# Half of a first MoE product by one level of Strassen, in batches 2 to 5 of an attention + MoE kernel

## The chip, the cores and the metric

The kernel runs on one core of a Trainium2 chip. The metric is device time in microseconds (us). A core has five engines with an instruction stream each: TensorE (matmuls; the profile calls it PE, and its weight loads PEld), VectorE (DVE), ScalarE (ACT), GpSimd (POOL) and SyncE (SP, which here only issues DMAs). TensorE writes into PSUM[...]; VectorE and ScalarE read it from there.

## The reference

```python
# q, k, v: (8, 12, 448, 64);  w_in: (768, 2048);  w_out: (2048, 768)
q_n, k_n = rmsnorm(q, g_q), rmsnorm(k, g_k)
scores = q_n @ k_n.T / sqrt(64)
attn = exp(scores - max); attn = attn / (sum(attn) + 1e-9)
x = (attn @ v), laid out as (8 * 448, 768)
h = x @ w_in
g = maximum(0.01 * h, h)
return g @ w_out                      # (3584, 768) float32
```

There are eight batches of 448 tokens. The change concerns `x @ w_in`, the first product.

## The kernel before

The attention of a batch is done in three units of four heads, 24 units in all (u = 0 to 23). A unit has four steps (d = 0 to 3): in step 0 the scores of one key tile, in steps 1 to 3 of two each. Step 0 also holds the `attn @ v` product of the unit before (`pv`), its row sums (`zc`) and the shift of the exponentials (a maximum on VectorE, a matmul, a small maximum on VectorE). Between the scores, TensorE is given items of the MoE products of an earlier batch from a queue, in proportion to their estimated cost; jobs for the other engines are handed out one after each item:

```python
def fill(u, d, jobs):
    ...                       # left: the steps until this batch's queue has to be empty
    debt[0] += total * WD[d] / left
    while queue and debt[0] >= queue[0][0] * 0.5:
        c, fn = queue.pop(0)
        fn()                          # one item: TensorE's matmuls
        debt[0] -= c
        if jobs:
            jobs.pop(0)()             # one job of another engine
    flush()                           # what items left to be emitted later
    for job in jobs:
        job()
```

A batch's items enter the queue in step 3 of units 6, 9, 12, and so on: those of batch b in unit 3b + 3. The jobs that matter here:

```python
if d == 0 and narrow(u - 1): job(zcol_inv, u - 1)          # ScalarE, then DMAs
if u + 4 < NU:               job(load, u + 4)              # q and k of a later unit (step 0)
if d == 1: job(prep_g, u + 1); job(prep_ssq, u + 2, ...) x2   # VectorE
if d == 2: job(prep_rinv, u + 2)                           # ScalarE
           job(prep_norm, u + 2, ...) x2                   # VectorE, waits for rinv
           job(prep_trd, u + 2)                            # DMA transpose
if d == 3: job(prep_sq, u + 3, ...) x2                     # ScalarE
```

(This list is shortened: the conditions on u are cut.)

A block of the first product is 128 of the 2048 features: six matmuls of 448 columns into one PSUM bank, then one activation on ScalarE. Four banks are passed around. The list `held` gives the first one free, and the semaphores see to it that its last reader is done:

```python
def aux(shape, dtype, name):
    if held:
        return held[0].pop(0)
    return psum.tile(shape, dtype, tag="aux", bufs=4, name=name)

def drop(bank):
    if held:
        held[0].append(bank)

def moe1(b, ft):                                   # an item "M", cost 1.13
    xt = xts[b]
    hps = aux([P, 512], FP32, "hps")
    for kt in range(KT):                           # KT = 6
        nc.tensor.matmul(hps[:, 0:S], win16[:, kt // 2, kt % 2, ts(ft, P)], xt[:, kt // 2, kt % 2],
                         start=(kt == 0), stop=(kt == KT - 1))
    prelu(b, gt[:, ft, ...], hps[:, 0:S])          # ScalarE
    drop(hps)
```

The second product (`g @ w_out`) already uses one level of Strassen (the functions `s1` to `s4` and `seven`). For the first product only the last two batches do: batch 6 for half of its blocks, batch 7 for all. There the seven products are numbered 1 to 7, and each is done for pairs s of output blocks, as six matmuls of 224 columns (half of the tokens). What a product leaves for the other engines is put off with `later` and emitted by `flush` at the start of the next item:

```python
def item(n, s):                                    # cost 0.575
    flush()
    ...
    if n == 1:
        mm(get(1, s), 1, s, x_b(b, 0, 0), True)
        later(lambda: copy(tmp["u"][:, s % 2], g[1, s][:, 0:S]))     # a copy to SBUF
    elif n == 2:
        mm(get(2, s), 2, s, x_b(b, 1, 0), True)                      # a bank of its own
        ...
    elif n == 4:
        mm(g[7, s], 4, s, xs[4], False)            # accumulates onto what VectorE left there
        later(lambda: out_(s, 1, 0, g[7, s][:, 0:S]))                # ScalarE
        later(lambda: drop(g[7, s]))
```

## Time and profile before

| | |
|---|---|
| time, median of 3 | 421.34 us (421.13 to 421.40) |
| span of the profiled execution | 420.3 us, 9568 instructions |
| granted TensorE clock, mean | 0.992 |
| first product, 448 columns, blocks outside the very first two (L362) | 612 matmuls |
| first product by Strassen, 224 columns (L564) | 252 matmuls |
| exponentials (L214) | 166, mean 1010 ns |
| activation of a block (L356) | 556 ns |

The profile's page gives busy time by engine and the chain that ended last; the trace behind it can be asked for busy time by stretch, for the waits, and for the instructions in order of time. In a line of the timeline the first number is the start in us from the beginning of the span, the second the length, then come engine, line of the kernel, operation, and output <- inputs with their shapes; "x6" means that six instructions are merged, and a bracket at the end tells how long the engine sat idle before it and what ended that. A line such as "DVE n L167 <- ACT rinv L161: 44.2, 15, 6.6" in the list of waits says that VectorE waited for ScalarE 44.2 us in total, 15 times, 6.6 us at the longest. The end of a matmul is modelled, so that consecutive matmuls overlap in the records: the distance from one start to the next is what one costs.

### The profile page before, as it was taken

What the parts mean: (1) busy time and instruction counts of PE and PEld (TensorE: products, weight loads), DVE (VectorE), ACT (ScalarE), POOL (GpSimd) and SP (SyncE); (2) the same over time, 40 slices, a digit from 0 to 9 for tenths busy, and PEclk for the clock granted to TensorE, in tenths of its full rate; (3) what the DMA queues carried; (4) which work ended last, traced back from release to release, by engine and by line L of the source; (5) the groups of instructions that cost most, each with busy time, mean ns of one, the idle gap of its engine ahead of it and who ended that gap; (6) DMA issues with size and microseconds to landing.
All of it is one profiled execution on the core that took longest, in us unless ns stands there. A gap on an engine that the chain in (4) does not pass through costs nothing.

```text
span 420.3 us, 9568 instructions
## 1 busy us (share of the span) xinstructions
PE 404.4 (96%) x3959; PEld 222.9 (53%) x3959; DVE 269.2 (64%) x440; ACT 303.6 (72%) x474; POOL 83.0 (20%) x75
## 2 busy tenths in 40 slices
PE   7977999999999999999999999999999999999995
PEld 6544444555445544555445544455445557558853
DVE  5788665787658736466448745467338787527762
ACT  5999878868987689867986779967986657653600
POOL 1958422300020111210121111120101101010000
PEclk9699999999999999999999999999999999999999
DMA  8999999889664795678565796578562460032023
GB/s 257 218 239 237 235 250 147 200 156 215 169 153 68 224 212 120 168 163 180 152 130 107 194 203 150 151 141 170 180 111 44 121 155 11 7 78 75 2 53 100
DMA packets 71951, 62.42 MB, mean 149 GB/s; under 512 B 36324, under 2 KB 67044, under 8 KB 71908
## 3 DMA queue, kind: packets, MB, share of 16 engines
q1 hardware_dynamic: 61312, 49.62, 47.2%
q0 software_dynamic: 10272, 11.80, 18.1%
q8 instruction: 31, 0.51, 0.5%
q10 hardware_dynamic: 324, 0.39, 0.3%
q14 instruction: 12, 0.10, 0.1%
HBM read 45.61 MB, written 11.01 MB: 135 GB/s over the span
## 4 chain that ended last, share of the span: by engine, by line
PE 83%; ACT 8%; DVE 6%; issue 1%; DMA 1%; SPq 0%; DVEq 0%; ACTq 0%
PE hps L362 27%; PE sT L195 8%; PE sT L340 6%; PE ma L444 5%; PE md L444 5%; PE mc L444 5%; ACT et L214 5%; PE bank L444 5%; PE bank L564 4%; PE op L403 3%; PE zc L283 3%; PE mb L444 3%; DVE n L167 2%; PE sT L444 2%; PE bank L403 1%
## 5 line engine op out<-in xcount | busy, mean ns | idle before, releaser
L214 ACT ACTIVATE et<-sT,eb 128x896 f16<-128x896 f32 x166 | 159.4, 1010 | 18.6 <-PE sT L195 16.9
L362 PE MATMUL hps<-xt,win 128*128 128x448 f16 x600 | 120.8, 353 | 0.2 <-DVE xt L349 0.2
L362 PEld LDWEIGHTS <-win 128*128 128x128 f16 x612 | 56.8, 98 | 58.2 <-issue 9.6
L320 POOL TENSOR_TENSOR xt<-x,rz 128x896 f16<-128x896 f32 x16 | 33.4, 2085 | 148.0 <-DMA rz<-zs 139.5
L356 ACT ACTIVATE gt<-hps 128x448 f16<-128x448 f32 x100 | 54.0, 556 | 6.1 <-PE hps L362 5.4
L167 DVE TENSOR_TENSOR n<-rq,rinv 128x896 f16<-128x896 f32 (+2 forms) x25 | 27.2, 1090 | 47.0 <-ACT rinv L161 44.2
L195 PE MATMUL sT<-qkT 64*64 64x448 f16 x664 | 53.2, 369 | 3.0 <-ACT et L214 1.9
L155 DVE TENSOR_REDUCE ssq<-sq 128x14 f32<-128x896 f32 (+2 forms) x49 | 50.3, 1058 | 1.6 <-ACT sq L144 1.6
L444 PEld LDWEIGHTS <-sa 128*128 128x128 f16 x352 | 32.8, 98 | 26.3 <-issue 6.1
L295 ACT COPY x<-sT 128x896 f32<-128x896 f32 x19 | 17.2, 906 | 36.4 <-DVE sT L245 36.4
L124 POOL DMA_DIRECT2D vt<-in_v_dram x24 | 18.2, 757 | 114.9 <-PE sT L340 107.4
L444 PEld LDWEIGHTS <-gt 128*128 128x128 f16 x264 | 25.2, 98 | 18.7 <-issue 2.1
L195 PEld LDWEIGHTS <-qkT 64*64 64x64 f16 x672 | 15.2, 105 | 36.8 <-issue 33.5
L340 PE MATMUL sT<-et,vt 64*64 64x448 f16 x532 | 28.5, 350 | 0.3
L403 PE MATMUL op<-wout,gt 128*128 128x384 f16 x160 | 28.4, 327 | 0.0
L232 DVE TENSOR_REDUCE sT<-sT 128x1 f32<-128x896 f32 x22 | 24.1, 1093 | 4.3 <-PE sT L195 4.3
L340 PEld LDWEIGHTS <-vt 64*64 64x64 f16 x672 | 20.7, 107 | 11.3 <-issue 1.7
L167 DVE TENSOR_TENSOR n<-rk,rinv 128x896 f16<-128x896 f32 (+2 forms) x26 | 26.1, 1009 | 0.0
L403 PEld LDWEIGHTS <-gt 128*128 128x128 f16 x192 | 17.6, 98 | 14.3 <-issue 3.0
L444 PE MATMUL ma<-wout,gt 128*128 128x384 f16 x128 | 23.5, 326 | 0.0
L425 DVE TENSOR_TENSOR sa<-gt 128x512 f16<-128x512 f16 (+1 forms) x15 | 8.2, 544 | 18.5 <-ACT gt L356 13.9
L144 ACT ACTIVATE sq<-rq 128x896 f32<-128x896 f32 (+2 forms) x18 | 16.3, 913 | 1.3 <-DMA rq<-in_q_dram 1.3
(135 smaller groups left out, 516.6 us busy)
## 6 DMA issues: line engine op xcount, KB each, us to landing
rq<-in_q_dram SPq DMA_DIRECT2D x24, 448.0 KB, 3.9
rk<-in_k_dram SPq DMA_DIRECT2D x24, 448.0 KB, 5.6
out_dram<-ost SPq DMA_DIRECT2D x52, 192.0 KB, 3.3
rz<-zs SPq DMA_DIRECT2D x76, 112.0 KB, 2.3
vt<-in_v_dram POOLq DMA_DIRECT2D x24, 224.0 KB, 5.1
win<-in_moe_w_in_dram POOLq DMA_DIRECT2D x8, 384.0 KB, 16.8
wout<-in_moe_w_out_dram POOLq DMA_DIRECT2D x2, 1536.0 KB, 29.7
out_dram<-ost SPq DMA_DIRECT2D x4, 96.0 KB, 2.1
```

Source lines behind the costliest of these rows:

```text
L124: nc.gpsimd.dma_start(vts[u % NV].rearrange("p a t d -> p a (t d)"), rows(v, u))
L155: nc.vector.tensor_reduce(buf(u, "ssq")[:, ti, :, c[0]:c[1]], buf(u, f"sq{ti}")[:, :, c[0]:c[1]], axis=AXL.X, op=ALU.add)
L167: nc.vector.tensor_tensor(buf(u, "n16")[:, ti, c[0]:c[1]].rearrange("p s a d -> p a s d"), src[:, :, c[0]:c[1]], buf(u, "rinv")[:, ti, :, ...
L195: nc.tensor.matmul(banks[a][64 * r:64 * r + 64, 0:S].rearrange("p (t x) -> p t x", t=NS), kT(u, r, a, t), qT(u, r, a), start=True, stop=True)
L214: nc.scalar.activation(s["et"][:, t], sT[:, :, 0:S], AF.Exp, bias=s["eb"], scale=1.0)
L232: nc.vector.tensor_reduce(s["spare"][:, 511:512], sT[:, :, 0:S], axis=AXL.XY, op=ALU.max)
L320: eng.tensor_tensor(xts[b][:, g], s["x32"], s["rz"], op=ALU.mult)
L340: nc.tensor.matmul(s["pv"][r][64 * a:64 * a + 64, 0:S], vts[u % NV][64 * r:64 * r + 64, a, t], s["et"][64 * r:64 * r + 64, t, a], start=(t ...
L356: nc.scalar.activation(dst, src, AF.Prelu, bias=0.0, scale=1.0, alpha=0.01)
L362: nc.tensor.matmul(hps[:, 0:S], win16[:, kt // 2, kt % 2, ts(ft, P)], xt[:, kt // 2, kt % 2], start=(kt == 0), stop=(kt == KT - 1))
L403: nc.tensor.matmul(op2[:, 0:HC], gt[:, ft, ds(col(t), P)], wout16[:, ft, ds(HC * half, HC)], start=(ft == 0), stop=(ft == FT - 1))
L444: nc.tensor.matmul(bank[:, 0:HC], a[:, f], b[:, f], start=(first and f == 0), stop=(f == HF - 1), skip_group_check=not first)
```

## The change

In batches 2 to 5 the first product of eight of the sixteen blocks (pairs 2 and 3, in both halves of the features) is done as seven products instead of eight. The aim is to take matmul work off TensorE. The four sums of weight blocks that this needs are made once, in unit 9, and used to the end; one of them overwrites a block of the weights in place, and the other three stand in the third buffers of q, k and their squares, so that from then on those have two buffers and the loads of q and k are issued in step 2 instead of step 0. In step 3 of units 9, 12, 15 and 18 VectorE makes four sums of x, for batches 2, 3, 4 and 5.

So as not to need SBUF buffers and more than four banks, a product's values are combined in PSUM: product 1 is copied by VectorE into a bank `g[6, s]`, onto which TensorE then accumulates products 6, 5 and 3, while product 2 is accumulated onto product 1's own bank; product 7's bank takes a sum from VectorE and then product 4. [...]

```diff
+    def written():
+        for i, x in enumerate(held[0]):
+            if any(x is y for y in full):
+                return held[0].pop(i)
...
     def load(u, engines=None):
-        raw[u] = [raws.tile([P, 2, NS, D], FP32, tag=name, name=name) for name in ("rq", "rk")]
+        raw[u] = [ring(raws, name, u in (2, 5, 8), [P, 2, NS, D], FP32, name) for name in ("rq", "rk")]
...
+        def mid(n, s):
+            flush()
+            hold()
+            if n == 1:
+                mm(get(1, s), 1, s, x_b(b, 0, 0), True)
+                later(lambda: g.__setitem__((6, s), written()))
+                later(lambda: nc.vector.tensor_copy(g[6, s][:, 0:S], g[1, s][:, 0:S]))
+            elif n == 7:
+                mm(get(7, s), 7, s, xs[b][3], True)
+                g["w", s] = opool.tile([P, S], FP32, tag="ost", name="w")
+                later(lambda: nc.vector.tensor_copy(g["w", s], g[7, s][:, 0:S]))
+            elif n == 2:
+                mm(g[1, s], 2, s, x_b(b, 1, 0), False)
+                later(lambda: out_(s, 0, 0, g[1, s][:, 0:S]))
+                later(lambda: drop(g[1, s], True))
+            elif n == 6:
+                mm(g[6, s], 6, s, xs[b][2], False)
+                later(lambda: vadd(g[7, s][:, 0:S], g[6, s], g["w", s]))
+            elif n == 5:
+                mm(g[6, s], 5, s, xs[b][1], False)
+                later(lambda: vadd(g["w", s], g[6, s], g["w", s]))
+                later(lambda: out_(s, 1, 1, g["w", s]))
+            elif n == 4:
+                mm(g[7, s], 4, s, xs[b][4], False)
+                later(lambda: out_(s, 1, 0, g[7, s][:, 0:S]))
+                later(lambda: drop(g[7, s], True))
+            else:
+                mm(g[6, s], 3, s, x_b(b, 1, 1), False)
+                later(lambda: out_(s, 0, 1, g[6, s][:, 0:S]))
+                later(lambda: drop(g[6, s], True))
...
+    MID = 2
+    MID_HALF = ("M", "M", (1, 2), (7, 2), "M", (2, 2), (6, 2), "M", (5, 2), (4, 2), (1, 3), (7, 3), (3, 2), (2, 3), "M", (6, 3),
+                "M", (5, 3), (4, 3), "M", (3, 3), "M")
...
-            for n, x, fs in ((len(items) - 7, 1, (s3, s4)),) if late else ((8, 0, (s1, s2)), (10, 0, (s3, s4)), (FT - 1, 1, (s1, s2)), (FT, 1, (s3, s4))):
+            for n, x, fs in ((len(items) - 7, 1, (s3, s4)),) if late else ((20, 1, (s1, s2)), (21, 0, (s1, s2)), (22, 1, (s3, s4)), (22, 0, (s3, s4))) if b >= MID else (
+                    (8, 0, (s1, s2)), (10, 0, (s3, s4)), (FT - 1, 1, (s1, s2)), (FT, 1, (s3, s4))):
...
-                    if u + 4 < NU:
+                    if u + 4 < NU and u < 7:
                         job(load, u + 4)
...
                         if u > 3:
                             job(prep_trd, u + 2)
+                        if u + 4 < NU and u >= 7:
+                            job(load, u + 4)
...
+                if u == 3 * MID + 3:
+                    n, tile_ = ((1, (raws, "rqb", 1)), (2, (raws, "rkb", 1)), (4, (prep_p, "sqb", 1)), (3, None))[d]
+                    job(win_sum, n, 1, tile_)
+                if fed(u, d) and MID < u // NQ <= LATE:
+                    for n in (3, 1, 2, 4):
+                        job(x_sum, u // NQ - 1, n)
                 if u == NU - 2 and d == 0:
-                    for n, tile_ in ((1, (raws, "rq", 3)), (2, (raws, "rk", 3)), (3, None), (4, (prep_p, "sq", 3))):
-                        job(win_sum, n, 1, tile_)
                     for n in (3, 1, 2, 4):
                         job(x_sum, LATE, n)
```

In `mm`, six matmuls of 224 columns are emitted; `out_` is the activation on ScalarE; `vadd` is an addition on VectorE, of which one operand lies in PSUM.

## The prediction

> **What bounds the kernel now.** I read the page's first part, then the busy time by stage, then the list of waits, then the timeline of one attention unit. First part of the page:
>
> ```profile
> PE 404.4 (96%) x3959; PEld 222.9 (53%) x3959; DVE 269.2 (64%) x440; ACT 303.6 (72%) x474; POOL 83.0 (20%) x75
> ```
>
> Busy time by stage (stretch, its length, then busy us of TensorE, weight loads, VectorE, ScalarE, GpSimd, granted clock, DMA):
>
> ```profile
> 150.00:200.00 50.00, 49.90 (x470) 24.86 (x469) 27.50 (x41) 41.59 (x67) 8.49 (x6) 1.00 0.73 167
> 200.00:250.00 50.00, 49.90 (x468) 25.44 (x467) 30.58 (x51) 39.13 (x62) 8.54 (x6) 1.00 0.68 155
> ```
>
> Batches 2 to 5 lie from 148 to about 340 us. TensorE is busy 49.9 of 50 us there: each microsecond of matmul removed is a microsecond gained, and each new microsecond of TensorE waiting is one lost. No slack of its own absorbs either. ScalarE is at about 80%, VectorE at 55 to 61%. From the list of waits (in us, times, longest):
>
> ```profile
> DVE n L167 <- ACT rinv L161: 44.2, 15, 6.6
> PE sT L195 <- ACT et L214: 1.9, 5, 0.5
> ```
>
> VectorE stands still up to 6.6 us in front of the normalization (`n`), because ScalarE's `rinv` comes late. Today this costs nothing: no matmul needs VectorE quickly there. TensorE waits for nothing of weight. The timeline of the last two steps of unit 12 (start, length, instruction):
>
> ```profile
> 185.54 0.57 PE L195 MATMUL sT<-qkT 64*64 64x448 f16 x8
> 186.03 1.91 ACT L214 ACTIVATE et<-sT,eb 128x896 f16<-128x896 f32 x2
> 187.82 0.33 ACT L160 ACTIVATE uu<-ssq,eps_t 128x28 f32<-128x28 f32 x1
> 188.17 0.23 ACT L161 ACTIVATE rinv<-uu 128x28 f32<-128x28 f32 x1
> 188.43 1.09 DVE L167 TENSOR_TENSOR n<-rq,rinv 128x896 f16<-128x896 f32 x1 [0.31 <-ACT rinv L161]
> 189.91 1.08 DVE L167 TENSOR_TENSOR n<-rk,rinv 128x896 f16<-128x896 f32 x1
> 190.98 0.95 ACT L144 ACTIVATE sq<-rq 128x896 f32<-128x896 f32 x1
> 192.54 1.09 DVE L232 TENSOR_REDUCE sT<-sT 128x1 f32<-128x896 f32 x1
> 193.67 0.29 DVE L234 TENSOR_TENSOR dg<-ident,sT 128x128 f16<-128x128 f16 x1
> 194.39 0.23 PE L244 MATMUL sT<-dg,onesp 128*128 128x64 f16 x2
> ```
>
> Read from it: `rinv` is finished 2.9 us after the step's score matmuls begin (188.40 - 185.54), the two normalizations take VectorE 1.0 us each, and `dg` is there 0.4 us (194.39 - 193.96) before TensorE reaches the matmul that needs it.
>
> [...]
>
> ```profile
> 350.33 1.30 PE L362 MATMUL bank<-xt,win 128*128 128x448 f16 x6
> 351.46 0.74 PE L564 MATMUL bank<-xt,win 128*128 128x224 f16 x6
> ...
> 388.09 0.74 PE L564 MATMUL bank<-xs,win 128*128 128x224 f16 x6
> 388.67 0.74 PE L564 MATMUL bank<-xs,ws 128*128 128x224 f16 x6
> ```
>
> Six matmuls of 448 columns take 1.13 us from start to next start (188 ns each), six of 224 take 0.575 us (96 ns): Strassen's halves lose almost nothing to their size. [...] before does so (four banks, one product block each), and TensorE has no wait for a block's activation worth listing. The change gives that rotation up.
>
> **The change, part by part.**
>
> Removed. Eight of a batch's sixteen blocks: 8 x 6 x 188 ns = 9.02 us. Added: 7 products x 2 pairs x 6 matmuls of 224 columns = 84 x 95.8 ns = 8.05 us. Gain 0.97 us a batch, **3.9 us** over four. Activations stay eight of 448 elements. The four weight sums (0.95 us each) move from unit 22, where they hid, to unit 9. VectorE gets, per batch, eight operations of 0.62 us (rows of the copy and of the additions in batches 6 and 7) and four sums of x of 0.50 us: 7 us in about 48, taking it to about 72%. As a total that is no bound; the order is what matters.
>
> To see the order I worked through the filling rule by hand arithmetic on its item costs: which product falls into which step of which unit, which jobs stand between, and which of the four banks each takes. For the kernel before it gives the item counts that the timeline shows. With (u, d) for unit and step, after the change:
>
> (10,2): product 6, block M, product 5; jobs `rinv`, `norm`, `norm`. (10,3): products 4 of pair 2, 1 and 7 of pair 3, then 3 and 2; jobs `sq`, `sq`. Unit 16 is the same. (13,2): products 5, 4, 1, 7. (13,3): 3, 2, M, 6. Unit 19 is nearly the same.
>
> Wait A, units 10 and 16. Product 7 of pair 3 can take only one bank: product 1 and its copy of pair 3 hold two, product 6's running bank of pair 2 the third. The fourth is product 7's of pair 2, freed when ScalarE has written out block (1,0). On ScalarE that stands behind the write-out of (1,1), two exponentials and a square; and (1,1) waits for VectorE's addition, emitted behind both normalizations. With T the start of step 2's scores: `rinv` T+3.0, normalizations T+5.0, addition T+5.55, write-out (1,1) T+6.05, exponentials T+7.85, square T+8.7, write-out (1,0) T+9.15. TensorE would be there at T+0.5+0.6+1.15+0.6+0.5+0.6+0.6 = T+4.55. Loss 4.6 us, twice: **9.2 us**. The loss lies on the path[...].
>
> Wait B, units 11 and 17, step 0: M, product 6, M. The second M gets the bank of the row sums `zc`, free only after ScalarE's copy out, exponential and logarithm: 2.7 us after the shift's matmul, against 1.8. 0.9 us twice: **1.8 us**.
>
> Wait C, units 13 and 19: product 7 of pair 3 again needs the bank of pair 2, here behind exponentials, `rinv` and one write-out: T+3.85 against T+2.3, 1.6 us. Then M in step 3 needs product 3's bank behind two exponentials and a square: 3.75 against 1.7 us after the step's start, 2.05 us. Twice, with 0.3 us at unit 14: **7.6 us**.
>
> Wait D, units 14 and 20: the sums of activations for the second product now begin after the last Strassen write-out, with `ssq` between: ready at T+6.0, and TensorE needs them at T+4.25. 1.7 us twice: **3.4 us**.
>
> Wait E, the sums of x before units 10, 13, 16, 19 are four VectorE operations ahead of the maximum that fixes the shift. At unit 13: 192.54 becomes about 193.8, the shift's matmul 195.25 instead of 194.39, 0.85 us; three such. At unit 10 the sum of weights in place and the one before it come first, and one TensorE item fewer lies in front: 3.5 us. **6.0 us**.
>
> Sum: -3.9 + 9.2 + 1.8 + 7.6 + 3.4 + 6.0 = +24.1, or 445. I choose **441**: the five were each worked with the other engines where before has them, and a stall in front lets ScalarE and VectorE catch up, so some of what follows should come out smaller.
>
> **Rivals.** (1) The matmul saving alone reaches the end: 421.3 - 3.9 = 417.4. For it: TensorE is at 99.8% in this stage, VectorE has 40% idle, and batch 6 runs half its blocks so already without a TensorE wait of note. Against: at batch 6 no normalization, square or load of a later unit stands in the queues, and its copies go to SBUF through another order. (2) Only the ownership of banks binds, because ScalarE reaches the write-out (1,1) later than I think and VectorE is done by then: A is 2.3 us each (ScalarE's exponentials, square and write-out alone), B and C stay, D and E vanish into slack; 421.3 - 3.9 + 4.6 + 1.8 + 7.6 = 431.4. (3) The loads: two buffers for q and k from unit 9 on, issued two steps later. A load lands in 4 to 6 us and is first read a whole unit of about 15 us afterwards, so 0. If it did bind, squares on ScalarE would wait for DMA, perhaps 2 us a unit, and 450 or more.
>
> **Range and chances.** Only the small gain is certain; the waits A and C are fixed by bank ownership alone to at least 2 x 2.3 + 7.3 = 12 us, which leaves 429. That is my lower end; 450 is the sum with half as much again in D and E. More than 2% faster (under 412.9) is beyond what the arithmetic removed can give: 1%. Within 2% (to 429.8) needs more than half of the waits to be absent: 11%. Slower by more than 2%: 88%.
>
> **What would show it.** Groups of 224-column matmuls up from 252 to 588 and 448-column blocks down from 612 or so to 420 on the product line, with 96 and 188 ns spacing: the gain. TensorE's busy share down to about 92%, with gaps of 3 to 5 us in front of product 7 in units 10 and 16 and 1.5 to 2 us in units 13 and 19, ended by ScalarE's write-out. ScalarE waiting about 2 us for the addition at the write-out (1,1) right before these. The shift's matmul waiting for `dg` at units 10, 13, 16, 19. If TensorE shows 49.9 of 50 us in these stages as before, my order of the queues is wrong, and the time will be near 417.

## The result, and the profile after

| | before | after |
|---|---|---|
| time, median of 4 | 421.37 us (421.13 to 422.67) | **464.50 us** (461.62 to 464.68) |
| ratio after / before, 95% interval | | **1.100** (1.095 to 1.105) |
| span of the profiled execution | 420.3 us | 462.9 us |
| TensorE busy | 404.4 us | 410.6 us |
| TensorE not busy (span less busy) | 15.9 us | 52.3 us |
| mean granted TensorE clock | 0.992 | 0.970 |

The change costs 10%. The direction and the waits had been foreseen; the size (441, at most 450) had not. One execution of a later kernel (tuned2, 447.9 us) counts as slow and is left out of its ratio.

The first part of the page of after, and its row of granted TensorE clock in 40 equal slices of the span (9 is 90% or more of full speed):

```profile
PE 410.6 (89%) x4103; PEld 240.0 (52%) x4103; DVE 301.6 (65%) x488; ACT 305.6 (66%) x474; POOL 83.6 (18%) x75
...
PEclk9899999999999789999989997999999999999999
```

Two things are to be read here. TensorE stands idle 36.4 us more (52.3 - 15.9). And it is *busy* 6.2 us more, although 3.9 us of matmul was taken away: some 10 us must have gone into matmuls that ran more slowly. The digits 7 and 8 in the middle of the clock row say where; before had 9 there throughout.

Busy time by stage (columns as before: stretch, length, TensorE, weight loads, VectorE, ScalarE, GpSimd, granted clock, DMA):

```profile
150.00:200.00 50.00, 43.37 (x395) 24.94 (x395) 25.22 (x41) 33.95 (x53) 5.67 (x4) 0.91 0.55 135
200.00:250.00 50.00, 41.34 (x417) 23.79 (x419) 32.18 (x51) 32.45 (x52) 7.75 (x5) 0.97 0.48 110
250.00:300.00 50.00, 41.93 (x424) 24.81 (x417) 29.65 (x47) 32.89 (x52) 8.60 (x6) 0.93 0.59 146
```

Where TensorE had 49.9 of 50 us it now has 41 to 43, and no other engine has taken its place: ScalarE has gone down to two thirds, VectorE stands at 50 to 64%. So no engine is the bound by its amount of work; the engines wait for each other in turn. The list of waits names them (us in total, times, longest):

```profile
PE bank L584 <- ACT gt L594: 11.6, 4, 5.8
...
PE sT L259 <- DVE dg L249: 9.1, 6, 3.9
...
ACT gt L594 <- DVE w L597: 7.7, 4, 4.1
```

L584 is a Strassen product, L594 its write-out on ScalarE, L597 VectorE's addition ahead of that. The wait for `dg`, of which nothing stood in the list before, is the shift of the exponentials. The timeline of unit 10 (around 150 to 170 us) shows both, first TensorE alone:

```profile
150.14 0.26 PE L259 MATMUL sT<-dg,onesp 128*128 128x64 f16 x2 [3.92 <-DVE dg L249]
150.22 2.75 PE L459 MATMUL md<-tw,gt 128*128 128x384 f16 x8
152.76 3.63 PE L377 MATMUL bank<-xt,win 128*128 128x448 f16 x12
...
163.77 0.74 PE L584 MATMUL bank<-xt,win 128*128 128x224 f16 x6
169.09 1.28 PE L584 MATMUL bank<-xs,win 128*128 128x224 f16 x6 [4.58 <-ACT gt L594]
170.16 1.32 PE L584 MATMUL bank<-xt,ws 128*128 128x224 f16 x6
```

then all engines in the stretch that ends in the second wait:

```profile
162.73 1.09 DVE L182 TENSOR_TENSOR n<-rq,rinv 128x896 f16<-128x896 f32 x1 [1.02 <-ACT rinv L176]
163.74 1.08 DVE L182 TENSOR_TENSOR n<-rk,rinv 128x896 f16<-128x896 f32 x1
164.74 0.62 DVE L597 TENSOR_TENSOR w<-bank,w 128x448 f32<-128x448 f32 x1
...
165.39 0.58 ACT L594 ACTIVATE gt<-w 128x448 f16<-128x448 f32 x1 [2.26 <-DVE w L597]
165.88 1.89 ACT L229 ACTIVATE et<-sT,eb 128x896 f16<-128x896 f32 x2
...
167.66 0.95 ACT L159 ACTIVATE sq<-rq 128x896 f32<-128x896 f32 x1
168.49 0.54 ACT L594 ACTIVATE gt<-bank 128x448 f16<-128x448 f32 x1
```

This is wait A link for link: `rinv`, two normalizations, the addition, the write-out of (1,1), two exponentials, a square, the write-out of (1,0), and only then product 7 of pair 3 at 169.09, 4.58 us late.

What the prediction had no term for stands in the TensorE lines. Six matmuls of 224 columns take 0.74 us in the records; after the wait they take 1.28 and 1.32. Eight of 384 columns take 2.75 us at 150.22, and 1.46 elsewhere in this trace; the twelve of 448 columns 3.63, elsewhere 2.43. For some microseconds after these waits of 3.92 and 4.58 us TensorE runs at about half speed: the granted clock is 0.59 from 150.1 to 156.3 us and 0.54 from 169.0 to 172.5, against 1.00 from 156 to 164.

### The profile page after: what moved, and what is told of

Its sections match the earlier page's. It is cut to its first block, busy times and chain, and to the rows that moved or that the text cites. A ratio compares the mean times of both kernels' runs of the same rounds, so it can differ in the third digit from the quotient of the medians.

```text
span 462.9 us, 9919 instructions
## 1 busy us (share of the span) xinstructions
PE 410.6 (89%) x4103; PEld 240.0 (52%) x4103; DVE 301.6 (65%) x488; ACT 305.6 (66%) x474; POOL 83.6 (18%) x75
## 5 line engine op out<-in xcount | busy, mean ns | idle before, releaser
L377 PEld LDWEIGHTS <-win 128*128 128x128 f16 x420 | 39.5, 99 | 42.6 <-issue 12.6
L377 PE MATMUL bank<-xt,win 128*128 128x448 f16 x240 | 51.8, 358 | 5.3 <-ACT gt L594 3.4
L310 ACT COPY x<-sT 128x896 f32<-128x896 f32 x19 | 17.2, 906 | 55.7 <-DVE sT L260 55.7
L182 DVE TENSOR_TENSOR n<-rq,rinv 128x896 f16<-128x896 f32 (+2 forms) x25 | 29.7, 1190 | 19.9 <-ACT rinv L176 17.0
L584 PEld LDWEIGHTS <-win 128*128 128x128 f16 x336 | 33.0, 101 | 16.5 <-issue 14.2
L459 PE MATMUL bank<-tw,sa 128*128 128x384 f16 x192 | 36.7, 342 | 5.4 <-DVE sa L443 5.4
L459 PEld LDWEIGHTS <-gt 128*128 128x128 f16 x264 | 26.1, 101 | 21.9 <-issue 6.1
L377 PE MATMUL hps<-xt,win 128*128 128x448 f16 x180 | 36.6, 353 | 0.2 <-DVE xt L364 0.2
L466 DVE TENSOR_TENSOR ost<-bank,ost 128x384 f32<-128x384 f32 x40 | 22.1, 553 | 15.6 <-PE bank L459 13.7
L247 DVE TENSOR_REDUCE sT<-sT 128x1 f32<-128x896 f32 x22 | 24.1, 1094 | 9.9 <-PE sT L210 9.9
L584 PE MATMUL bank<-xs,win 128*128 128x224 f16 x156 | 20.1, 269 | 11.6 <-ACT gt L594 11.6
L584 PEld LDWEIGHTS <-ws 128*128 128x128 f16 x252 | 24.0, 100 | 10.3 <-issue 8.1
L459 PE MATMUL bank<-wout,gt 128*128 128x384 f16 x144 | 27.4, 334 | 0.2 <-ACT gt L594 0.2
```

The costliest lines, as they stand in the source:

```text
L182: nc.vector.tensor_tensor(buf(u, "n16")[:, ti, c[0]:c[1]].rearrange("p s a d -> p a s d"), src[:, :, c[0]:c[1]], buf(u, "rinv")[:, ti, :, ...
L247: nc.vector.tensor_reduce(s["spare"][:, 511:512], sT[:, :, 0:S], axis=AXL.XY, op=ALU.max)
L459: nc.tensor.matmul(bank[:, 0:HC], a[:, f], b[:, f], start=(first and f == 0), stop=(f == HF - 1), skip_group_check=not first)
L466: nc.vector.tensor_tensor(dst, g[name][:, 0:HC], src, op=ALU.add)
L584: nc.tensor.matmul(bank[:, HX * i:HX * i + HX].rearrange("p (t x) -> p t x", t=NS), w, x[:, kt], start=start, stop=(kt == HK - 1), skip_gr ...
```

## The experiments

All are compared with before on the same chip (421.6 us in the first two groups, 422.64 and 421.96 in the last two). Most are single executions, and the same kernel scatters by up to 5 us where TensorE waits much (461.6 to 464.7 for after, 440.4 to 445.7 for tuned2). Time alone therefore does not settle a difference of less than about 5 us; I read such pairs by the waits and by TensorE's idle and busy time. "Idle" is span less TensorE's busy time, of the profiled execution: 15.9 us before, 52.3 after. Line numbers shift from kernel to kernel by the lines that were put in.

### Are the loads to blame? (loads_only)

```diff
-    MID = 2
+    MID = 6
```

No batch uses the new scheme, but q, k and their squares have two buffers from unit 9 on and the loads come two steps later.

> Only the two-buffer rings and the later loads of q and k are kept; batches 2 to 5 run plain blocks, and the weight sums are made in unit 21. Theory 'order' (the time went into TensorE waits made by the order of the VectorE and ScalarE queues and by bank ownership, plus half clock after long waits): 421 us, within 1 us of before. Rival 'loads' (q and k arrive late with two buffers): 430 us or more, with ScalarE's squares waiting for DMA.

Measured, over four executions: 425.02 us, ratio 1.009 (1.006 to 1.012); idle 18.7 us. A small miss: 3.4 us instead of none. Hardly any of it is a wait for a load: one square waited once for its load, 1.2 us, and TensorE has new waits of 1.17 us (at 275.92) and 1.31 us (at 343.09, where this variant makes the weight sums) for `dg`. Ahead of the first, in loads_only:

```profile
268.85 2.07 POOL L335 TENSOR_TENSOR xt<-x,rz 128x896 f16<-128x896 f32 x1 [9.06 <-ACT gt L371]
269.25 2.62 DVE L182 TENSOR_TENSOR n<-rq,rinv 128x896 f16<-128x896 f32 x1 [5.64 <-ACT rinv L176]
271.79 1.08 DVE L182 TENSOR_TENSOR n<-rk,rinv 128x896 f16<-128x896 f32 x1
```

The normalization takes 2.62 us beside GpSimd's multiplication and 1.08 behind it. In before, GpSimd's multiplication was all but over when VectorE began (266.86 + 2.07 = 268.93 against 268.78), and the normalization took 1.10. In loads_only the one comes 2.0 us later and the other only 0.5, so that they overlap by 1.5 us more, and the normalization takes 1.5 us longer. Rival (3), 450 or more through loads, falls: the loads' part is at most 3.5 us.

### What do the sums cost by themselves? (sums_only)

```diff
-        if b >= MID:
+        if late:
```

The sums of weights and of x are made as in after, but batches 2 to 5 compute plain blocks (four of a batch's sixteen from a sum instead of the block of weights that was overwritten, so their values are others; the amount of work is that of before plus the sums). A second line gives the items of the second product the place that they have in before.

> The sums of weights and of x are made where the change makes them, but batches 2 to 5 run plain blocks; one sum still overwrites weights that plain blocks then use, so four of sixteen blocks are computed from other weights than the reference's, with the same amount of work. Theory 'order': the shift's matmul waits about 3.5 to 3.9 us in unit 10 and 0.7 to 1.2 us in units 13, 16 and 19, and the clock is at half for some 2.5 us of extra time after the first: about 430 us. Rival 'products' (all of the loss comes with the Strassen products themselves): 421 to 423 us.

Measured: 429.96 us; idle 21.2. Waits for `dg`: 3.03, 0.64, 1.41, 0.46 and 0.65 us. As expected. The idle time rose by 5.3 us where wait E had 6.0; TensorE's busy time rose by 2.6 us although no matmul was added; 1.6 of them are the twelve matmuls behind the 3.03 us wait (4.03 us instead of 2.43).

### Banks or order? (pairs_apart, early, light_add)

pairs_apart begins pair 3 only after the last product of pair 2, so that no product 7 waits for pair 2's bank:

```diff
-    MID_HALF = ("M", "M", (1, 2), (7, 2), "M", (2, 2), (6, 2), "M", (5, 2), (4, 2), (1, 3), (7, 3), (3, 2), (2, 3), "M", (6, 3),
+    MID_HALF = ("M", (1, 2), (7, 2), "M", (2, 2), (6, 2), "M", (5, 2), (4, 2), "M", (3, 2), (1, 3), (7, 3), "M", (2, 3), (6, 3),
```

> The changed kernel with the items of pair 3 begun only after product 3 of pair 2, with blocks between, so that product 7 of pair 3 no longer takes the bank just left by product 4. Theory 'order': the waits of product 7 for ScalarE (4.6 and 5.8 us, 0.6 twice) and of the block in units 13 and 19 (1.6 and 1.8) go, with about 3 us of half clock; the waits on VectorE behind the normalizations stay in part: 445 to 452 us. Rival 'VectorE is full' (its added 32 us are what TensorE waits for, in whatever order): 460 us or more.

Measured: 458.87 us; idle 47.1. Between the two, a miss for both: the waits in front of product 7 are gone, and others stand in their place. TensorE's lines in pairs_apart:

```profile
172.66 2.33 PE L377 MATMUL bank<-xt,win 128*128 128x448 f16 x6 [2.54 <-ACT zs L315]
...
275.28 1.28 PE L584 MATMUL bank<-xs,ws 128*128 128x224 f16 x6 [3.23 <-DVE bank L597]
```

A plain block now waits 2.54 us for the bank of the row sums, twice, and product 5 waits 2.32, 3.23 and 1.65 us for VectorE's addition behind product 6 (its line in the list is `DVE bank L597`).

early lets what a product leaves for VectorE and ScalarE be emitted at once and not at the next item, so that it stands ahead of the job handed out next (a normalization):

```diff
-                    items.append((0.575, lambda w=w: item(*w)))
+                    items.append((0.575, lambda w=w: (item(*w), None if late else flush())))
```

> The changed kernel with one difference: what a Strassen product of batches 2 to 5 leaves for VectorE and ScalarE is emitted right behind its matmuls, before the job handed out after it, so that write-outs no longer stand behind a square, nor the additions behind a normalization handed out after the same item. Theory 'order': product 7 of pair 3 in units 10 and 16 waits 2.5 to 3.5 us instead of 4.6 and 5.8, product 5 in unit 13 and 19 not at all, the sums of activations in units 14 and 20 some 1 us less: 453 to 459 us. Rival 'VectorE is full': no difference beyond 2 us from 464.5.

Measured: 455.56 us; idle 45.7. The time is within the expected range. The two waits of A went from 4.58 and 5.79 to 2.73 and 3.14 us; those for the sums of activations (2.53 and 3.30 us) did not get shorter, against the expectation. What remains of them is near the 2.3 us that rival (2) gave to ScalarE's exponentials, square and write-out alone. So by this run A was about half VectorE's order and half the bank behind ScalarE.

light_add cuts the operations that VectorE makes for the products from 448 to 64 columns and leaves the rest of them out; the order stays. The copy `w` of product 7 goes to a tile of its own (`wfix`) instead of one of the buffers `ost`:

```diff
-                later(lambda: vadd(g[7, s][:, 0:S], g[6, s], g["w", s]))
+                later(lambda: few(g[7, s], g[6, s], g["w", s]))      # 64 columns; so for all four
```

> The changed kernel with its copies and additions of batches 2 to 5 on VectorE cut to 64 of 448 columns (the rest of the sums is left out, so the values of these blocks are not the reference's); the instructions, their order and their waits are the same, each is about 0.4 us shorter. Theory 'order': the waits behind rinv, normalizations, squares and exponentials stay, each shorter by 0.4 to 0.8 us: 456 to 461 us. Rival 'VectorE time' (the length of the added operations is what TensorE waits for): 445 us or less.

Measured: 466.33 us; idle 52.3, as in after; VectorE busy 289.8 instead of 301.6. Not a microsecond came back, a miss even for the theory of order, which had left some gain to it. Product 5's waits (1.92, 0.80 and 1.21 us in after) are gone, and those of product 7 and for `dg` are longer by 2.7 us in sum (13.2 + 10.2 against 11.6 + 9.1). In this order, what a product waits for is not how long VectorE adds, but behind what the addition stands. light_both also leaves the sums of x out (products take x itself):

> As the run with short additions, and the sums of x for batches 2 to 5 left out as well: products 4 to 7 stream x itself. Theory 'order': the waits for the shift in units 10, 13, 16 and 19 go with the half clock after the first, those of product 7 and of the blocks stay: 447 to 452 us. Rival 'VectorE time': 435 us or less.

Measured: 456.68 us, some 5 us above the range of the theory of order and far above the rival's; idle 46.9. The 5.4 us of idle time that came back are mostly wait E, found from the other side (sums_only: 5.3). The waits for product 7 (6.05 us twice) stayed. So in this order the length of VectorE's additions is no cause; the sums of x are, through the place in which they stand.

### The half speed (probe, probe_short)

To see it without Strassen, eight waits are put into before: a chain of VectorE additions, and a dummy matmul of 448 columns that reads its result.

```diff
+            nc.tensor.matmul(hps[:, 0:S], onesp, dmy[:, 0:S], start=True, stop=True)
...
+            for i in range(n):
+                nc.vector.tensor_tensor(dmy[:, 0:S], dmy[:, 0:S], src, op=ALU.subtract)
```

> The kernel before, with TensorE made to wait eight times for a chain of VectorE additions of 448 fp16 elements (1, 3, 5, 7, 9, 4, 6, 12 after the first), at eight places some 15 us apart. Each wait should be about 1.0 us plus 0.4 us per addition: 1.4 to 6 us, some 28 us in all. Theory 'clock': the matmuls after a wait of more than about 2.5 us run at half speed for some us, 1.5 to 2.5 us lost each time, and those after the waits of 1.4 and 2.2 us do not: about 459 us. Rival 'no clock effect' (the doubled spacing after the gaps in the changed kernel has another cause, such as the banks): spacing stays at 188 ns, about 449 us.

Measured: 485.51 us, with waits of 2.76 to 9.28 us; they came out longer than meant, 45.8 us in sum, which is why the time is above the expectation. All eight were followed by half speed, so a wait alone does it, without the banks of the new scheme. TensorE in probe after the shortest wait, then the same twelve matmuls in the next step:

```profile
155.28 0.51 PE L366 MATMUL hps<-dmy,onesp 128*128 128x448 f16 x1 [2.76 <-DVE dmy L377]
155.58 4.02 PE L368 MATMUL hps<-xt,win 128*128 128x448 f16 x12
...
160.03 2.44 PE L368 MATMUL hps<-xt,win 128*128 128x448 f16 x12
```

TensorE's busy time is 421.6 us, 17.2 more than before; less 1.5 us for the dummies and divided by eight, **2.0 us are lost after each wait**, on top of the wait. probe_short does the same with short waits:

> The kernel before with eight short TensorE waits, between about 1 and 3 us: the next block's bank is first written from the activation of the block just done (five places), or from a chain of one or two VectorE additions on it (three). Theory 'clock': matmuls behind waits under 2 us keep 188 ns, those behind waits over 2.7 us start at about 375 ns; between, it goes either way. About 440 us. Rival 'no threshold' (every wait costs some clock): 188 ns nowhere right after a wait.

Measured: 441.63 us. Of eight waits (1.90, 1.84, 1.62, 1.83, 1.54, 2.26, 2.05, 1.83) only one was followed by half speed. TensorE's busy time rose by 4.8 us; less 1.5 us for the dummies and 2.0 for that one, some 0.2 us are left for each of the seven other waits.

```profile
272.90 0.35 PE L366 MATMUL hps<-dmy,onesp 128*128 128x448 f16 x1 [2.26 <-DVE dmy L377]
273.09 3.65 PE L368 MATMUL hps<-xt,win 128*128 128x448 f16 x12
...
312.29 0.36 PE L366 MATMUL hps<-dmy,onesp 128*128 128x448 f16 x1 [2.05 <-DVE dmy L379]
312.49 2.43 PE L368 MATMUL hps<-xt,win 128*128 128x448 f16 x12
```

To see how this depends on the length of the wait I counted all waits of 0.8 us and more between 120 and 420 us in after and in the sixteen kernels of this study, and how many have matmuls at half speed within 5 us behind them (a slow stretch is put down to the last of these waits ahead of it):

| TensorE's wait | count | followed by half speed |
|---|---|---|
| 0.8 to 1.2 us | 50 | 1 |
| 1.2 to 2.1 us | 54 | 7 |
| 2.1 to 2.8 us | 19 | 9 |
| 2.8 to 3.5 us | 12 | 10 |
| above 3.5 us | 23 | 23 |

Below 3.5 us it went either way, above in every case. None of the eight in the first two rows stands alone. Six (tuned2's 1.63 us at 231.29 for one) have another wait, of 0.33 to 1.80 us, 2.2 to 2.5 us ahead. The other two, 1.03 us in tuned4 and 1.36 us in tuned5, are followed by waits of 0.77 and 0.52 us within 2.4 us, and the 28 matmuls of `attn @ v` behind them take 2.68 and 2.83 us instead of 1.49 to 1.52. So it seems that several together did it; the same three waits in tuned2 (0.96, 0.77, 0.52) did not. After has five waits beyond 2.5 us in batches 2 to 5 (3.92, 4.58, 2.56, 5.79, 2.85), and all five were followed by half speed; five times 2.0 are the 10 us that its busy time had too much.

### Can another order take the loss back?

sums_moved emits the sums of x behind the small maximum of the shift instead of ahead of it, and the weight sums a step earlier:

```diff
-                if fed(u, d) and MID < u // NQ <= LATE:
-                    for n in (3, 1, 2, 4):
-                        job(x_sum, u // NQ - 1, n)
+                            if u % NQ == 1 and MID <= u // NQ - 1 < LATE:    # in step 0, behind the small maximum
+                                for n in (3, 1, 2, 4):
+                                    x_sum(u // NQ - 1, n)
```

> The changed kernel with the four sums of x moved behind the shift's small maximum in units 10, 13, 16 and 19, and the sums of weights one step earlier. Theory 'order': the waits for the shift in these four units (3.9, 1.2, 0.7 and 1.2 us) and the half clock after the first (2.5 us) go, the rest stays: 455 to 457 us. Rival: the sums come back as waits of the first Strassen products, because VectorE has to do them in any case: 462 us or more.

Measured: 464.88 us; idle 51.8. The waits for `dg` fell from 9.1 to 3.4 us, and nothing was gained. The list of waits of sums_moved:

```profile
PE bank L584 <- DVE bank L597: 11.9, 4, 4.2
PE bank L584 <- ACT gt L594: 8.7, 2, 4.8
```

The first line is new in this size: product 5 waits for VectorE's addition behind product 6, 1.8 to 4.2 us, once in each batch. The time is in the rival's range, but its reason, that VectorE is at work on the sums in any case, is not what the trace shows. Ahead of these waits VectorE stands still; unit 10 of sums_moved:

```profile
158.88 0.62 DVE L661 COPY w<-bank 128x448 f32<-128x448 f32 x1 [4.16 <-DMA out_dram<-ost]
...
160.42 0.62 DVE L597 TENSOR_TENSOR bank<-bank,w 128x448 f32<-128x448 f32 x1
...
161.09 0.73 PE L584 MATMUL bank<-xs,ws 128*128 128x224 f16 x6 [3.49 <-DVE bank L597]
```

The scheme was to need no SBUF buffers, but product 7's copy `w` takes one of the four buffers `ost`, which also hold the outputs on their way to DRAM and the sums of x. It waits until the DMA of an output has freed one: 4.16, 5.04, 2.47 and 3.25 us in the four batches. The same waits of `w` (2.89, 3.36 and 2.22 us) stand ahead of product 5 in pairs_apart and ahead of the longest TensorE waits of tuned2, tuned4, tuned5, tuned6 and tuned7 below; after itself has two, of 1.47 and 2.03 us. So in these kernels the buffer is a rival to the order of the queues for part of the loss. In the order of after, light_add, with `w` in a tile of its own, gained nothing; in another order no run gives `w` a buffer of its own and keeps all of the work.

tuned2 changes all the orders at once, and leaves no work out: pair 3 apart in the first half and otherwise mixed, leftovers emitted at once, sums of x and of activations where VectorE is free, and on ScalarE `rinv` between the two exponentials of step 2 and the squares as the last of step 3:

```diff
+                    if d == 2 and 3 * MID + 3 <= u < NU - 2:
+                        two = st[u]["sT"]
+                        st[u]["sT"] = two[:1]
+                        ex(u)                       # the first exponential
+                        prep_rinv(u + 2)
+                        st[u]["sT"] = two[1:]
...
+                if d == 3 and 3 * MID + 3 <= u < NU - 3:
+                    prep_sq(u + 3)
```

> All of the work of the changed kernel in another order: leftovers before jobs, sums of x behind the shift, sums of weights earlier, rinv between the two exponentials of step 2, the row sums' logarithm before the copy out of the pv slot, squares last in step 3, pair 3 begun after product 3 of pair 2, the sums of activations right behind their blocks. VectorE and ScalarE do as much as in the changed kernel. Theory 'order': most waits go, no wait is long enough to halve the clock: 418 to 428 us. Rival 'VectorE is full': 440 us or more.

Measured: ratio 1.050 (1.043 to 1.056), 440.4 to 445.7 us in three executions; idle 36.6, the longest wait 2.75 us. About 20 us of the 43 come back by order alone, and 21 to 24 are left: far from the 418 to 428 expected. The rival's reason for that, a full VectorE, is tested by tuned2_light, where VectorE's operations are cut to 64 columns and the sums of x left out as above:

> The reordered kernel (same order as the one measured before at 445) with the additions cut to 64 columns and the sums of x for batches 2 to 5 left out. If order and VectorE time together are the whole loss, the matmul saving comes through: 418 to 424 us. If ScalarE and the four banks still bind on their own: 430 us or more.

Measured: 436.22 us (before: 422.64); idle 29.6. A third of the remaining idle time went, most of it stayed. What went need not be VectorE's work: here too `w` is a tile of its own, and product 5's waits of 2.75 and 1.09 us behind the waits of `w` in tuned2 are gone. The run does not tell the two apart. tuned3 keeps the work and gives the sums of x to GpSimd (the wait that its expectation gives to product 6 is product 5's):

> The reordered kernel with the sums of x for batches 2 to 5 made by GpSimd, all of the work done. Theory 'VectorE time' for what is left: product 6's wait of 2.8 us in unit 10 and its like in unit 16 go: 438 to 442 us. Rival 'shared access' (GpSimd at work slows VectorE, as a normalization took 2.6 instead of 1.1 us beside GpSimd's multiplication in the loads-only run): 445 us or more.

Measured: 444.85 us (before: 422.64); idle 37.7, GpSimd busy 114.5. No gain; among the waits is one of 4.06 us right at the new sums, of which GpSimd makes two in 4.09 us. What tuned2 still shows is a normalization of 3.02 us beside GpSimd:

```profile
191.79 2.07 POOL L335 TENSOR_TENSOR xt<-x,rz 128x896 f16<-128x896 f32 x1 [7.71 <-ACT rinv L176]
191.79 3.02 DVE L182 TENSOR_TENSOR n<-rq,rinv 128x896 f16<-128x896 f32 x1 [0.64 <-ACT rinv L176]
```

The last group moves that apart, step by step. tuned4 puts ScalarE's `zcol_inv`, whose result the multiplication needs, right behind the logarithm, so that GpSimd comes earlier; tuned5 also takes VectorE's `ssq` of units 11, 14, 17 and 20 into step 0; tuned6 is tuned5 with `rinv` back behind both exponentials; tuned7 is tuned6 with the multiplication on VectorE instead of GpSimd from unit 9 on.

```diff
+                            if 3 * MID + 3 <= u < NU - 1:            # tuned4, in step 0
+                                zcol_inv(u - 1)
...
-                    if d == 1:                                       # tuned5: where ssq is handed out
+                    if d == (0 if 3 * MID + 3 <= u and u % NQ == 2 else 1):
...
+                if d == 2 and 3 * MID + 3 <= u < NU - 1:             # tuned7
+                    job(xmul_sb, u - 1)                              # VectorE, in place of GpSimd
```

> The reordered kernel with the reciprocal of the row sums made right behind its logarithm, so that the DMAs of rz and GpSimd's multiplication come some 2 us earlier and end before the normalizations. Theory 'shared access' (VectorE stands still while GpSimd multiplies: 3.0 instead of 1.1 us for a normalization, 2.3 instead of 0.45 for the scaling of qkT): the waits of the second product's items for VectorE in units 12, 14, 18, 20 (1.3 to 1.8 us, eight of them) mostly go: 434 to 440 us. Rival 'order alone': 443 us or more.

> As the run before, and the sums of squares of units 11, 14, 17, 20 made in step 0 instead of step 1, out of the way of the sums of activations. Theory: the waits for those in units 14 and 20 (1.7 us, with 1.6 us behind) go: 430 to 437 us. Rival: they come back at the shift's small maximum or at the Strassen additions: no gain on the run before.

> As the run before, but rinv again behind both exponentials of step 2, so that the normalizations start about 0.9 us later, behind GpSimd's multiplication. If GpSimd still overlaps the normalizations in the run before, this one is faster (427 to 434 us); if not, it is slower by 2 to 4 us, because the write-outs behind the normalizations come later.

> As the run before, but from unit 9 on VectorE makes the multiplication of x instead of GpSimd (1.1 us more of VectorE in each unit, no GpSimd work beside it). Theory 'shared access': VectorE loses nothing by it, as it stood still for about 2 us each time: 426 to 434 us, at or below the run before. Rival 'VectorE time': 5 us or more above the run before.

| kernel | us (before: 421.96) | TensorE idle | TensorE busy |
|---|---|---|---|
| tuned4 | 439.41 | 31.2 | 406.4 |
| tuned5 | 435.83 | 25.8 | 408.3 |
| tuned6 | 440.34 | 33.3 | 405.3 |
| tuned7 | 440.20 | 31.9 | 406.5 |

tuned4 falls within the scatter of tuned2 in time; by its waits, the ones of 1.3 to 1.8 us in units 12 and 18 (3.1 us in sum) are gone. tuned5 has the least idle time of the reordered kernels, and the shortest time by its single execution. tuned6's idle time is 7.5 us above tuned5's; product 5's waits for VectorE rose by as much (10.3 - 2.8 us): the place of `rinv` matters. tuned7 gives VectorE 14 multiplications of 1.08 us, 15.2 us in sum, and its busy time rises by 7.6 only (305.7 against 298.1 in tuned6); its other operations became 7.6 us shorter, 2.3 of them the normalizations, now all of 1.08 us. TensorE waits no longer than in tuned6. So GpSimd's multiplication took from VectorE about half of what it spared it; but the drop to 426 or so that I had hoped for did not come. The page of tuned5:

```profile
PE 408.3 (94%) x4103; PEld 238.0 (55%) x4103; DVE 298.9 (69%) x488; ACT 307.1 (71%) x474; POOL 83.2 (19%) x75
...
PEclk9899999999999988999998998999999999999999
```

Against before, tuned5 is idle 9.9 us more and busy 3.9 more. As 3.9 us of matmul is saved in it too, 7.8 us went into slower matmuls; 6 to 7 of these I find in the records: behind its longest wait (2.81 us), behind a pair of waits of 0.61 and 1.24 us, and behind the three of 1.36, 0.77 and 0.52 us. These are the three dips in the middle of its clock row. The rest of its idle time is small waits all over the stage, which I did not take apart further. None of these kernels beats before, and none could by more than 3.9 us (0.9%), the whole matmul saving.

## Why the prediction was right in kind and wrong in size

The terms against the trace (TensorE's waits in batches 2 to 5, in us):

| term | predicted | measured | |
|---|---|---|---|
| matmul saving | -3.9 | -3.9 | 588 and 420 matmuls, six in 0.74 and 1.30 us, as before |
| A, product 7 in units 10, 16 | 9.2 | 10.4 | 4.58 and 5.79 |
| B, second M in units 11, 17 | 1.8 | 1.7 | 0.83 twice |
| C, units 13, 14, 19 | 7.6 | 8.0 | product 7 and M 4.9; 3.1 already in front of product 5 |
| D, sums of activations, units 14, 20 | 3.4 | 5.4 | 2.56 and 2.85 |
| E, sums of x ahead of the shift | 6.0 | 6.9 | 3.92, 1.18, 0.65, 1.18 |
| waits without a term | 0 | 4.6 | units 12, 16, 18 |
| half speed after waits | 0 | 9 to 10 | |
| sum | +24.1 | +42 to 43 | span: 462.9 - 420.3 = 42.6 |

**What held.** The gain, to the tenth. The order of the queues, worked out by hand, and through it each of the five waits, within 2 us, and in its place but for C. That C's sum fits is in part luck: its product 7 waited 0.61 us instead of 1.6 in units 13 and 19, while product 5, for which no wait was foreseen, waited 1.92 and 1.21 us for VectorE. "ScalarE waiting about 2 us for the addition at the write-out (1,1)" was 2.26 us in unit 10 and 4.15 in unit 16. Rival (1), 417.4, is out: the saving is there and is paid for ten times over. Rival (2), 431.4, is out as a whole (E and D did not vanish), but early showed that its 2.3 us for the bank alone were about right for half of A. Rival (3) is out by loads_only.

**The step that failed.** The sum of +24.1 us falls 18.5 short. Of these, 9 to 10 us are matmuls at half speed, against the prediction's "each new microsecond of TensorE waiting is one lost"; 4.6 are waits that it had no term for; 4.4 are its five waits, longer than worked out. The two terms at zero are taken up below. The last step then went the wrong way: "I choose 441: ... a stall in front lets ScalarE and VectorE catch up, so some of what follows should come out smaller." The measured waits came out larger, 37.0 against 28.0 us. A reason can be read from wait A, though no run tests it. Behind TensorE's waits the others stand in a ring: TensorE waits for ScalarE, which waits for VectorE, which waits for ScalarE's `rinv`, which stands behind exponentials that wait for TensorE's scores. In this ring the stalls gave the others no time to catch up. The upper end of 450, "the sum with half as much again in D and E", rested on the same step.

**Term mis-sized at zero: TensorE after a wait.** A microsecond of waiting was put down as a microsecond. It is about that only while the wait is short (some 0.2 us more for each of seven, 1.54 to 2.05 us, in probe_short); a long one costs 2.0 us more (probe, 2.76 to 9.28 us), five times in after. Before's trace could not show it in this stage: between 148 and 340 us its list of waits has no line of TensorE. By the count above, the predicted 4.6 us of A, twice, lie where all 23 waits were followed by half speed, and the 3.5 us of E in unit 10 at the edge of that row; 3 x 2.0 us would have been 6 of the missing 10. But the count gives no length below which one is safe: 2.56 and 2.85 us in after and 2.26 us in probe_short were followed by half speed too, and so were eight waits of 1.0 to 1.6 us with others close to them.

**Term mis-sized at zero: VectorE beside GpSimd.** In D, in A of unit 16 and in the waits without a term, VectorE's own operations were longer than in the rows of before that the prediction used. After, unit 16:

```profile
276.73 2.86 POOL L335 TENSOR_TENSOR xt<-x,rz 128x896 f16<-128x896 f32 x1 [9.65 <-ACT rinv L176]
...
277.57 2.97 DVE L182 TENSOR_TENSOR n<-rk,rinv 128x896 f16<-128x896 f32 x1
...
280.47 0.61 DVE L597 TENSOR_TENSOR w<-bank,w 128x448 f32<-128x448 f32 x1
```

The normalization ends 0.95 us after GpSimd's multiplication does (280.54 against 279.59), as in loads_only (271.87 against 270.92) and tuned2 (194.81 against 193.86): it seems to have stood still and then run most of its usual 1.08 us. These 1.9 us are most of the 2.2 us by which VectorE's addition, and with it product 7, came later than in unit 10, counted from the score matmuls of step 2. The normalizations take 2.97 us here, 2.62 in loads_only and 3.02 in tuned2, against 1.08 to 1.10 alone; in tuned7, without GpSimd's multiplication, all take 1.08. The prediction took VectorE's durations from unit 12 of before, where the two do not meet, and then moved VectorE's work by microseconds. Between 148 and 340 us before's own trace has two meetings of more than 0.15 us, in which the normalization takes 1.48 and 1.70 us and again ends 0.95 us after GpSimd's multiplication:

```profile
156.66 2.08 POOL L320 TENSOR_TENSOR xt<-x,rz 128x896 f16<-128x896 f32 x1 [7.91 <-DMA rz<-zs]
158.21 1.48 DVE L167 TENSOR_TENSOR n<-rq,rinv 128x896 f16<-128x896 f32 x1 [6.63 <-ACT rinv L161]
...
236.70 2.08 POOL L320 TENSOR_TENSOR xt<-x,rz 128x896 f16<-128x896 f32 x1 [8.46 <-ACT et L214]
...
238.03 1.70 DVE L167 TENSOR_TENSOR n<-rq,rinv 128x896 f16<-128x896 f32 x1 [0.31 <-ACT rinv L161]
```

The two waits for `dg` in units 12 and 18, 1.08 us each, have another origin: the shorter list of items brings the sums of the second product one item forward, ahead of the shift's maximum. The order of the items, worked out by hand, held that, but it was not followed to the shift.

**Still open:** which orders make up the last 14 us that tuned5 has over before (10 of waits, 8 of slower matmuls, less 3.9); how much of that is `w` waiting for a buffer; and what decides, for a wait between 2.1 and 3.5 us, whether the clock falls, which no run shows.

## What to carry to other kernels

Where TensorE is full and the other engines' queues are interleaved by hand, a change that saves 1% of the matmuls but lets TensorE's banks depend on two engines in turn must first be followed through the queues: here the dependence cost, not the length of the added work (cutting VectorE's additions to a seventh gave back nothing in the order of after). Follow the buffers too: here a copy that shares its buffers with the outputs waited up to 5 us for their DMAs. As an estimate from the count above (31 of 33 waits of 3 us or more were followed by half speed, 11 of 22 between 2 and 3 us) and from the 2.0 us of probe, put a TensorE wait of 3 us or more down at its length plus 2 us, and one of 2 to 3 us at its length plus 1. And when work moves on VectorE, look at what GpSimd does at the new time; a duration read from the old trace holds only for the old neighbours (here 1.08 us alone and up to 3.02 beside GpSimd).

## What the runs showed of the hardware that was not expected

- After a wait TensorE may run at about half speed for some us (12 matmuls of 448 columns in 3.65 us instead of 2.43 in probe_short; granted clock 0.59 from 150.1 to 156.3 us in after): in 19 of 31 cases between 2.1 and 3.5 us and in 23 of 23 above, at a cost of about 2.0 us each (the mean in probe); eight waits of 1.0 to 1.6 us did it too, each with another within 2.5 us.
- VectorE and GpSimd delay each other: a fp32 normalization begun beside GpSimd's multiplication takes 1.5 to 3.0 us instead of 1.1 and ends 0.95 us after it (twice in before, four times in after), GpSimd's own took 2.86 us instead of 2.07 in unit 16 of after, and in tuned2 a multiplication by a column, of fp16 in place, took 2.27 us beside GpSimd's and otherwise 0.45.
- Taking 12 us of work from VectorE (light_add) moved the end of the kernel by nothing that can be seen, while all of the work in another order (tuned2) moved it by about 20 us.
